# First feature and first key subtracted from a head's others, and 480 of 512 columns multiplied

## The chip, the cores and the metric

The kernel runs on one core of a Trainium2 chip. The metric is the device time of one execution in microseconds, the median of several runs. The core has TensorE (PE: matmuls, with weight loads in their own row, PEld), VectorE (DVE), ScalarE (ACT), GpSimd (POOL) and SyncE (SP, which here only issues transfers). They run side by side and wait for each other through semaphores.

## The reference

For 2048 tokens of 512 features, `x`, two branches are computed and mixed by a gate `g = sigmoid(x . gate_w)`: `g * a + (1 - g) * b`.

Branch a is a linear attention with 32 heads of 16 features, whose feature map is a pair of softmaxes:

```python
pq = jnp.einsum("bhsd,hdf->bhsf", q, w_phi)          # the same for pk
phi_q = jnp.concatenate([_softmax(pq, axis=-1), _softmax(-pq, axis=-1)], axis=-1)
kv = jnp.einsum("bhsf,bhsd->bhfd", phi_k, v)
z  = jnp.einsum("bhsf->bhf", phi_k)
o = num / den                                        # phi_q kv / (phi_q z + 1e-6), then @ wo
```

Branch b lets each of 32 heads choose one of 16 keys twice (`s1 = q1 . k1`, `s2 = q2 . k2`, the largest of each 16), which names one of 256 experts. The softmax over a single choice is 1, so the branch is `sum over heads of gelu(x . u[e]) * v[e]`.

Two facts of this arithmetic matter here. A softmax over the 16 features of a head does not change when one number is subtracted from all 16, and neither does the place of the largest of 16 scores. And q, k and the scores are linear in the weights: `x @ (w_q w_phi)`, `x @ (w_k w_phi)`, `x @ (w_q key)`.

## The kernel before

**Precision.** A matmul in the format fp32r keeps only the high part of an fp32 number, so each operand is split into a high and a low part (`h`, `l`), and one product is three matmuls: high by high, high by low, low by high (`mm3`, L52 to L57). With 512 input features in four chunks of 128, one product of a tile of 128 tokens with 512 columns is 12 matmuls that add up in one PSUM bank. `proj` (L116) makes one such product.

**Weights.** The features are folded into the weights once. `fold_k` (L225) multiplies `w_k` by `w_phi`, block by block, and `fold_turn` turns the result into `wah`, `wal`; late in the second stage `fold_q` (L207) writes the folded `w_q` over them. Both read the tile `wp`, which holds the 32 matrices `w_phi` in pairs as 32 x 32 blocks. `score_w` (L295) multiplies `w_q` of branch b by the two key tables in the tile `kp`; after a transpose by DMA the result lies in `sh`, `sl`: 1024 columns, two halves of 32 heads x 16 keys.

**Stages.** (1) Loads, folding of k, the first values. (2) k and v of the 16 tiles of tokens, and the sum `kv` over all tokens (`kvacc`). Tiles 0 to 4 and 15 are computed directly (`kproj`, `vproj`). Tiles 5 to 14 are taken in twos, with sums and differences of operands prepared on GpSimd (`Sums`), so that fewer products are needed; there the products are made by `prod` (L464), two chunks at a time, and the k of the odd tile of each two takes two calls with the folded weights (L493, L529). Between them lie the 16 calls of `score_w`, whose weights stream in from HBM. (3) Folding of q, the denominators (`z_final`). (4) One turn for each tile (`turned`, from tile 2 on): two products for the scores of the next tile (`front_s`), one for q (`front_q`), one of 258 columns for the experts and the gate (`front_p`), the masks of the chosen keys (`mid_mask`), the numerators (`mid_num`), and 18 matmuls of the output product (`back_mm`), dealt out in portions (`back_some`).

**What follows a product.** VectorE reads q and k from PSUM (`softmax_diffs`, L119): maximum and minimum over the 16 features of each head, then two differences, written to SBUF; ScalarE takes the exponential. For the scores, `best` (L729) finds the maximum of each 16 and writes a mask of where it is; the mask is transposed by DMA (`turn_eq`) and read by `mid_mask`. In all of these a head's 16 features, or keys, lie next to each other: column = 16 * head + feature.

**Order.** Every engine executes its instructions in the order in which the code issues them (`manual_schedule`); nothing is reordered. PSUM has four banks for products (`mm_bank`), taken in turn; a product can begin when the reader of the product four before it is done.

Of the kernel before, what the change touches and what calls it, by code (L numbers as in the profile page):

```python
# [16 lines left out]
ALU = mybir.AluOpType  # L17
AX = mybir.AxisListType
PSUM = bass.MemoryType.PSUM

P = 128
S = 2048
D = 512
NT = S // P
NK = D // P
H = 32
F = 16
# [7 lines left out]
def mix_kernel(ctx, tc, xT, wqT, wkT, wv, wphi, wo, wq, kk, ug, ev, cst, out):  # L35
    nc = tc.nc
    pe, dve, act, pool, sp = nc.tensor, nc.vector, nc.scalar, nc.gpsimd, nc.sync
# [11 lines left out]
        act.copy(hi, src)  # L49
        dve.tensor_tensor(lo, src, hi, op=ALU.subtract)  # L50

    def mm3(o, pairs, first=True, last=True):  # L52
        n = len(pairs)
        for i, (ah, al, bh, bl) in enumerate(pairs):
            pe.matmul(o, ah, bh, start=(first and i == 0), stop=False)  # L55
            pe.matmul(o, ah, bl, start=False, stop=False)  # L56
            pe.matmul(o, al, bh, start=False, stop=(last and i == n - 1))  # L57

    kvb = per.tile([P, 8, 32], F32, name="kvb")
    cs = per.tile([P, 160], F32, name="cs")  # L60
# [13 lines left out]
    def x_of(t):  # L74
        first = max(f for f in SEC if f <= t)
        return tuple(xt[i, first][:, t - first] for i in range(2))
# [6 lines left out]
    sh = per.tile([P, NK, 1024], F32R, name="sh")  # L83
    sl = per.tile([P, NK, 1024], F32R, name="sl")
    eh = per.tile([P, 2, D], F32R, name="eh")
    el = per.tile([P, 2, D], F32R, name="el")
    wah = per.tile([P, NK, D], F32R, name="wah")
    wal = per.tile([P, NK, D], F32R, name="wal")
# [18 lines left out]
    kp = per.tile([P, 2, 2, 32], F32, name="kp")  # L107
# [5 lines left out]
    def xs(t, k):  # L113
        return tuple(m[:, k, :] for m in x_of(t))

    def proj(o, t, wh, wl, c0, c1, ks=range(NK)):  # L116
        mm3(o, [(*xs(t, k), wh[:, k, c0:c1], wl[:, k, c0:c1]) for k in ks], ks[0] == 0, ks[-1] == NK - 1)

    def softmax_diffs(p, d, st, step=lambda: None):  # L119
        p3 = p.rearrange("p (h f) -> p h f", f=F)  # L120
        d4 = d.rearrange("p (h s f) -> p h s f", s=2, f=F)
        mx, mn = st[:, 0:32], st[:, 32:64]
        dve.tensor_reduce(mx, p3, axis=AX.X, op=ALU.max)
        step()
        dve.tensor_reduce(mn, p3, axis=AX.X, op=ALU.min)
        step()
        dve.tensor_tensor(d4[:, :, 0, :], p3, mx.unsqueeze(2).to_broadcast([P, H, F]), op=ALU.subtract)
        step()
        dve.tensor_tensor(d4[:, :, 1, :], mn.unsqueeze(2).to_broadcast([P, H, F]), p3, op=ALU.subtract)
        step()  # L130

    g64 = lambda a: a.rearrange("p (g f) -> p g f", f=F)
# [11 lines left out]
    wp = w1.tile([P, NK, 32], F32, bufs=1, name="wp")  # L144
# [14 lines left out]
    def x_high(t, ks=slice(0, NK)):  # L159
        (dve.tensor_copy if t < 3 else act.copy)(x_of(t)[0][:, ks], rawx[t][:, ks])  # L160
# [5 lines left out]
    def x_split(t, ks=slice(0, NK)):  # L166
        x_high(t, ks)
        x_low(t, ks)
# [7 lines left out]
    class Sums:  # L176
        h = ((gh, gl), x_of(NT - 1))
# [71 lines left out]
    phis, vs, pks, wsP, stk, joins = {}, {}, {}, {}, {}, []  # L249
# [19 lines left out]

    def kproj(t):  # L270
        pks[t] = mm_bank(f"pk{t}")
        proj(pks[t], t, wah, wal, 0, D)

    def k_exp(t):
        act.activation(phis[t], phis[t], AF.Exp)  # L275
# [56 lines left out]
    def front_s(t, half):  # L332
        e = st8[t]
        e[half] = mm_bank(f"s{half}_{t}")
        proj(e[half], t, sh, sl, 512 * half, 512 * half + 512)

    pool.memset(kvb, 0.0)
    tab = w1.tile([P, 1], F32, bufs=1, name="tab")
# [26 lines left out]
        split(wbh[:, k, :], wbl[:, k, :], rawv[:, k, :])  # L365
    act.dma_start(kp, kk)
    act.dma_start(cs, cst)
    x_split(1)
    dve.tensor_tensor(t2r, rawv[:, 2:4], rawv[:, 0:2], op=ALU.subtract)
    act.copy(t1r, rawv[:, 0:2])  # L370
# [90 lines left out]
            pool.tensor_tensor(t2l, t2r, t2h, op=ALU.subtract)  # L461
            pool.tensor_tensor(t4l, by4(t4r), t4h, op=ALU.subtract)

    def prod(o, left, right, first):  # L464
        for i, ((ah, al), (bh, bl)) in enumerate(zip(left, right)):
            for j, (x_, w_) in enumerate(((ah, bh), (ah, bl), (al, bh))):
                pe.matmul(o, x_, w_, start=(first and i + j == 0), stop=(i == 1 and j == 2),  # L467
                          skip_group_check=True)

    pair_of = lambda h, l, k: [(h[:, k], l[:, k]), (h[:, k + 1], l[:, k + 1])]  # L470
    b11, b21, b22 = pair_of(wah, wal, 0), pair_of(wah, wal, 2), pair_of(wbh, wbl, 2)
# [3 lines left out]
    tile_of = lambda t, k: [xs(t, k), xs(t, k + 1)]  # L475
    behind = None
    for t in range(5, NT - 1, 2):
        n = t + 1
        more = [u for u in (t + 4, t + 5) if u < NT]
        for u in more:  # L480
            x_load(u)
        if t == NT - 5:
            rawu = [spare(ug[:, 0:2], "rawu0", [P, 2, NU])]
        elif t == NT - 3:
            rawu.append(spare(ug[:, 2:4], "rawu1", [P, 2, NU]))
            rawe = [spare(ev[:, 0], "rawe0", [P, D])]
        if behind:
            k_diffs(behind)
        for u in (t + 2, t + 3):
            if u < NT - 1 and u not in (7, 9):  # L490
                x_low(u)
        a = pks[t] = mm_bank(f"pk{t}")
        prod(a, tile_of(t, 0), b11, True)  # L493
        b = mm_bank(f"pu{t}")
        act.copy(b, a)
        if 5 < t < NT - 3:
            Sums.add(t + 2)
        if t == 5:
            (j1, tp), = joins
            joins.clear()  # L500
            tj1 = wa_.tile([P, D], F32, tag="wtj", bufs=1, name="wtj1")
            join_tp(j1, tp, tj1)
            score_planes(2)
            load_wq()
            load_wq()
            join_end(j1, tj1)
            Sums.add(t + 2)
        elif t < NT - 3:
            join_all()
        else:  # L510
            (j6, tp), = joins
            joins.clear()
            tj6 = wa_.tile([P, D], F32, tag="wtj", bufs=1, name="wtj6")
            join_tp(j6, tp, tj6)
        e = tr_bank(f"pe{t}")
        prod(e, sums(0, 2), b1, True)
        prod(b, sums(1, 0), b2, False)
        c = mm_bank(f"pv{t}")
        act.copy(c, b)
        if t == 5:  # L520
            k_exp(4)
            k_sum(4)
            k_mult(4)
            x_high(9)
            (j2, tp), = joins
            joins.clear()
            tj2 = wa_.tile([P, D], F32, tag="wtj", bufs=1, name="wtj2")
            join_tp(j2, tp, tj2)
        prod(a, tile_of(t, 2), b21, False)  # L529
        k_diffs(t)  # L530
        if behind:
            k_exp(behind)
            k_sum(behind)
            k_mult(behind)
        score(2, 5 < t < NT - 3)
        if t == NT - 3:
            rawq = stage(wqT, "rawq")
            score_planes(7)
        elif t > 5:
            load_wq()  # L540
            load_wq()
        for u in (t - 3, t - 2):
            kvacc(u)
        vn, vt = v_tile(n), v_tile(t)
        if t > 5:
            act.copy(vn, by16(e))
            k_exp(t)
            k_sum(t)
        prod(b, sums(0, 0), b3, False)
        d = pks[n] = mm_bank(f"pk{n}")  # L550
        act.copy(d, b)
        if t == 5:
            join_high(j2, tj2)
            score_planes(3)
            act.copy(vn, by16(e))
            Sums.high(7, (0,))
            k_exp(t)
            x_low(9)
        prod(c, sums(1, 2), b22, False)
        if t == 5:  # L560
            Sums.high(7, (1,))
        if t == NT - 3:
            x_split(NT - 1)
        dve.tensor_tensor(vt, by16(c), vn, op=ALU.add)
        dve.tensor_tensor(vn, by16(b), vn, op=ALU.add)
        if t == 5:
            k_sum(t)
        o2 = d.rearrange("p (c n) -> p c n", c=2)
        prod(o2, tile_of(n, 2), b4, False)
        if t + 3 < NT:  # L570
            if t > 5:
                Sums.high(t + 2)
            Sums.low(t + 2)
            if t == 5:
                join_low(j2, tj2)
        if t == 7:
            for i in range(2):
                x_parts(i, 11)
        for u in more if n < NT - 4 else ():
            if u != 9:  # L580
                x_high(u)
        k_mult(t)
        behind = n
    t = NT - 1
# [36 lines left out]
    def step(t, n=1):  # L621
        for _ in range(n):
            if t in chains and next(chains[t], None) is None:
                del chains[t]
# [47 lines left out]

    def front_q(t):
        pq = mm_bank(f"pq{t}")
        proj(pq, t, wah, wal, 0, D)
        st8[t]["pq"] = pq

    def soft_in(t, step=lambda: None):
# [51 lines left out]
    def best(t, half):  # L730
        e = st8[t]
        if half == 0:
            e["eq"] = w2.tile([P, 1024], BF16, tag="eq", name=f"eq{t}")
        p3 = e[half].rearrange("p (h f) -> p h f", f=F)
        mx = w2.tile([P, 32], F32, tag="mx", name=f"mx{half}_{t}")
        dve.tensor_reduce(mx, p3, axis=AX.X, op=ALU.max)  # L736
        dve.tensor_tensor(e["eq"][:, 512 * half:512 * half + 512].rearrange("p (h f) -> p h f", f=F), p3,  # L737
                          mx.unsqueeze(2).to_broadcast([P, H, F]), op=ALU.is_equal)

    def turn_eq(t):  # L740
        e = st8[t]
# [332 lines left out]
    for a in range(NT - 1):  # L1074
        n, b, z = a + 1, a - 1, a - 2
# [61 lines left out]
    a, b, z = NT - 1, NT - 2, NT - 3  # L1137
# [140 lines left out]
```

## Time and profile before

| | |
|---|---|
| median of 3 runs | 366.96 us (366.78 to 367.57) |
| profiled execution | 367.09 us |
| its span, first to last instruction | 365.3 us |
| TensorE, matmuls | 358.8 us busy, 98% of the span |
| VectorE | 318.5 us, 87% |
| ScalarE | 256.7 us, 70% |
| GpSimd | 206.6 us, 57% |
| granted TensorE clock | 0.999 |

Matmuls are pipelined: a listed matmul of 512 columns lasts about 0.39 us, but the next one starts about 0.23 us after it, so the start-to-start distance is what a matmul costs. A row of a timeline reads: start, duration, engine, line, operation, output<-inputs, shape; in brackets the idle time before it and what ended that. A row of waits reads: engine, its tile and line, what it waited for, then microseconds in total, number of times, the longest. In a group of instructions, "x128 | 50.4, 394 | 0.0" is count, total busy us, mean ns of one, idle us before them.

### The profile page before, as it was taken

What the parts mean: (1) busy time and instruction counts of PE and PEld (TensorE: products, weight loads), DVE (VectorE), ACT (ScalarE), POOL (GpSimd) and SP (SyncE); (2) the same over time, 40 slices, a digit from 0 to 9 for tenths busy, and PEclk for the clock granted to TensorE, in tenths of its full rate; (3) what the DMA queues carried; (4) which work ended last, traced back from release to release, by engine and by line L of the source; (5) the groups of instructions that cost most, each with busy time, mean ns of one, the idle gap of its engine ahead of it and who ended that gap; (6) DMA issues with size and microseconds to landing.
All of it is one profiled execution on the core that took longest, in us unless ns stands there. A gap on an engine that the chain in (4) does not pass through costs nothing.

```text
span 365.3 us, 8628 instructions
## 1 busy us (share of the span) xinstructions
PE 358.8 (98%) x3404; PEld 282.2 (77%) x3404; DVE 318.5 (87%) x639; ACT 256.7 (70%) x455; POOL 206.6 (57%) x205
## 2 busy tenths in 40 slices
PE   7999999999999999999999999999999999999996
PEld 3766667777778878887888888888888888888764
DVE  3679999999968889999999799699899899699791
ACT  4586577977566666695786876866769787667882
POOL 1079989988938947446337355634734635636130
PEclk9999999999999999999999999999999999999999
DMA  7868787459693112243471344263344245145233
GB/s 254 321 237 304 241 274 248 137 210 309 206 247 99 57 38 51 39 100 45 101 117 43 88 86 90 57 104 65 80 86 102 50 111 101 46 88 129 31 100 117
DMA packets 75752, 47.57 MB, mean 130 GB/s; under 512 B 67264, under 2 KB 68160, under 8 KB 73408
## 3 DMA queue, kind: packets, MB, share of 16 engines
q1 hardware_dynamic: 74848, 46.15, 46.8%
q10 hardware_dynamic: 864, 0.87, 0.9%
q8 instruction: 27, 0.44, 0.5%
q14 instruction: 13, 0.11, 0.1%
HBM read 26.43 MB, written 4.19 MB: 84 GB/s over the span
## 4 chain that ended last, share of the span: by engine, by line
PE 86%; ACT 5%; POOL 3%; DMA 2%; DVE 2%; issue 1%; SPq 0%; POOLq 0%; ACTq 0%; DVEq 0%
PE po L889 9%; PE s L55 7%; PE s L56 7%; PE s L57 7%; PE pk L467 5%; PE po L896 5%; PE pu L467 4%; PE ws L300 4%; PE pq L55 4%; PE pq L56 4%; PE pq L57 4%; PE oT L776 2%; PE kvacc L291 2%; PE pp L55 2%; PE pp L56 2%; PE pp L57 2%
## 5 line engine op out<-in xcount | busy, mean ns | idle before, releaser
L728 POOL TENSOR_TENSOR d<-d,st 128x512 f32<-128x512 f32 x30 | 32.6, 1106 | 49.3 <-DVE st L721 48.1
L699 POOL TENSOR_TENSOR w<-d,zb 128x512 f32<-128x512 f32 x32 | 41.2, 1310 | 18.7 <-ACT d L693 18.7
L55 PE MATMUL s<-sh,xh 128*128 128x512 f32 x128 | 50.4, 394 | 0.0
L56 PE MATMUL s<-sl,xh 128*128 128x512 f32 x128 | 49.9, 389 | 0.0
L57 PE MATMUL s<-sh,xl 128*128 128x512 f32 x128 | 49.8, 389 | 0.0
L757 ACT COPY pl<-d 128x1024 uint16<-128x1024 uint16 x32 | 33.3, 1046 | 18.7 <-POOL d L728 18.7
L768 ACT COPY ptb<-tp 128x1024 uint16<-128x1024 uint16 x32 | 41.7, 1370 | 0.4 <-DMA tp<-pl 0.4
L284 POOL TENSOR_TENSOR d<-d,st 128x1024 f32<-128x1024 f32 x16 | 32.6, 2036 | 8.5 <-ACT d L275 6.5
L844 POOL TENSOR_TENSOR cf<-cf,px 128x256 f32<-128x256 f32 x15 | 11.1, 741 | 33.6 <-DVE cf L840 31.8
L55 PEld LDWEIGHTS s<-sh,xh 128*128 128x128 f32 x128 | 24.0, 188 | 5.3 <-issue 0.4
L57 PEld LDWEIGHTS s<-sh,xl 128*128 128x128 f32 x128 | 24.0, 188 | 5.1
L56 PEld LDWEIGHTS s<-sl,xh 128*128 128x128 f32 x128 | 24.0, 188 | 4.8
L55 PE MATMUL pq<-wah,xh 128*128 128x512 f32 x64 | 25.2, 393 | 0.0
L57 PE MATMUL pq<-wah,xl 128*128 128x512 f32 x64 | 24.9, 390 | 0.0
L56 PE MATMUL pq<-wal,xh 128*128 128x512 f32 x64 | 24.9, 389 | 0.0
L703 DVE TENSOR_REDUCE st<-d 128x32 f32<-128x512 f32 x32 | 20.5, 678 | 3.6 <-ACT d L693 3.5
L164 DVE TENSOR_TENSOR xl<-xr,xh 128x512 fp32r<-128x512 f32 (+2 forms) x17 | 21.7, 1292 | 1.7 <-ACT xh L160 1.6
L737 DVE TENSOR_TENSOR eq<-s,mx 128x512 bf16<-128x512 f32 x32 | 22.1, 692 | 1.1
L736 DVE TENSOR_REDUCE mx<-s 128x32 f32<-128x512 f32 x32 | 21.8, 680 | 0.2 <-PE s L57 0.2
L707 DVE TENSOR_REDUCE st<-w 128x32 f32<-128x512 f32 x32 | 20.5, 676 | 0.9 <-POOL w L699 0.9
L279 DVE TENSOR_REDUCE st<-d 128x64 f32<-128x1024 f32 x16 | 19.4, 1210 | 1.8 <-ACT d L275 1.6
L927 ACT COPY ot<-po 128x512 f32<-128x512 f32 x15 | 8.7, 589 | 16.3 <-PE po L896 14.8
(271 smaller groups left out, 1097.1 us busy)
## 6 DMA issues: line engine op xcount, KB each, us to landing
wq<-wq SPq DMA_DIRECT2D x16, 1024.0 KB, 5.2
xr<-xT SPq DMA_DIRECT2D x15, 256.0 KB, 5.1
y<-ot SPq DMA_DIRECT2D x15, 256.0 KB, 2.0
rawk<-wkT SPq DMA_DIRECT2D x1, 1024.0 KB, 6.8
rawq<-wqT SPq DMA_DIRECT2D x1, 1024.0 KB, 6.8
rawu<-ug SPq DMA_DIRECT2D x2, 258.0 KB, 5.5
rawv<-wv ACTq DMA_DIRECT2D x2, 256.0 KB, 4.7
rawv<-wv SPq DMA_DIRECT2D x2, 256.0 KB, 6.0
```

The lines of the kernel that those rows point to most:

```text
L55: pe.matmul(o, ah, bh, start=(first and i == 0), stop=False)
L56: pe.matmul(o, ah, bl, start=False, stop=False)
L57: pe.matmul(o, al, bh, start=False, stop=(last and i == n - 1))
L284: pool.tensor_tensor(g64(d), g64(d), b64(st[:, 128:192]), op=ALU.mult)
L467: pe.matmul(o, x_, w_, start=(first and i + j == 0), stop=(i == 1 and j == 2), skip_group_check=True)
L699: pool.tensor_tensor(hs(e["w"], i), hs(e["ph"], i), hs(zb, i), op=ALU.mult)
L728: eng.tensor_tensor(g64(d)[:, gs_], g64(d)[:, gs_], r[:, gs_].unsqueeze(2).to_broadcast([P, 32, F]), op=ALU.mult)
L736: dve.tensor_reduce(mx, p3, axis=AX.X, op=ALU.max)
L737: dve.tensor_tensor(e["eq"][:, 512 * half:512 * half + 512].rearrange("p (h f) -> p h f", f=F), p3, mx.unsqueeze(2).to_broadcast([P, H, F] ...
L757: act.copy(pl, e["ph"][:, halves[i]].bitcast(U16).rearrange("p (c j) -> p j c", j=2))
L768: act.copy(p16[:, t % 2, :, 4 * i:4 * i + 4, :], st8[t]["tp"][i].rearrange("p (j g) n -> p j g n", j=2))
L889: pe.matmul(po, a, b, start=(i == 0), stop=False)
```

## The change

The tile `wp` and the key table `kp` are altered on GpSimd right after they are loaded, ahead of the folds: the first feature (key) of each head is subtracted from the head's other 15 and is itself set to zero (`from_first`). The folded weights of q, k and the scores then have a column of zeros for each head, and every other column is the difference to it.

The heads are interleaved in twos, so that the two zero columns of two heads lie side by side: column = 32 * pair + 2 * feature + head in the pair. The host writes `w_phi` and the keys in that order, and VectorE reads PSUM through a rearranged view with a step of two (`heads`); what it writes to SBUF keeps the old order, and so does everything behind it.

`live` selects the 480 columns that are not zero: 16 runs of 30, with two columns left out between them. In each accumulation the first matmul still takes all 512, which writes the zeros; the others take 480, in the moving operand and in the output. This holds for `front_s`, `front_q`, `kproj`, and the two `prod` calls with the folded weights of an odd tile.

```diff
-    def mm3(o, pairs, first=True, last=True):
+    def mm3(o, pairs, first=True, last=True, live=lambda a: a):
         n = len(pairs)
         for i, (ah, al, bh, bl) in enumerate(pairs):
-            pe.matmul(o, ah, bh, start=(first and i == 0), stop=False)
-            pe.matmul(o, ah, bl, start=False, stop=False)
-            pe.matmul(o, al, bh, start=False, stop=(last and i == n - 1))
+            whole = first and i == 0
+            f = (lambda a: a) if whole else live
+            pe.matmul(f(o), ah, f(bh), start=whole, stop=False, skip_group_check=True)
+            pe.matmul(live(o), ah, live(bl), start=False, stop=False, skip_group_check=True)
+            pe.matmul(live(o), al, live(bh), start=False, stop=(last and i == n - 1), skip_group_check=True)
+
+    def from_first(w):
+        g = w.rearrange("p a (f i) -> p a f i", i=2)
+        pool.tensor_tensor(g[:, :, 1:], g[:, :, 1:], g[:, :, 0:1].to_broadcast([P, 4, F - 1, 2]), op=ALU.subtract)
+        pool.memset(g[:, :, 0:1], 0.0)
+
+    def live(a):
+        return a.rearrange("p (g f) -> p g f", f=2 * F)[:, :, 2:]
+
+    def heads(a):
+        return a.rearrange("p (g f i) -> p g i f", f=F, i=2)
+
+    twice = lambda a: a.rearrange("p (g i) -> p g i", i=2)
+    spread = lambda a: twice(a).unsqueeze(3).to_broadcast([P, F, 2, F])
...
     def softmax_diffs(p, d, st, step=lambda: None):
-        p3 = p.rearrange("p (h f) -> p h f", f=F)
-        d4 = d.rearrange("p (h s f) -> p h s f", s=2, f=F)
+        p4 = heads(p)
+        d5 = d.rearrange("p (g i s f) -> p g i s f", i=2, s=2, f=F)
...
-        dve.tensor_reduce(mx, p3, axis=AX.X, op=ALU.max)
+        dve.tensor_reduce(twice(mx), p4, axis=AX.X, op=ALU.max)
...
-        dve.tensor_tensor(d4[:, :, 0, :], p3, mx.unsqueeze(2).to_broadcast([P, H, F]), op=ALU.subtract)
+        dve.tensor_tensor(d5[:, :, :, 0, :], p4, spread(mx), op=ALU.subtract)
...
-        proj(pks[t], t, wah, wal, 0, D)
+        proj(pks[t], t, wah, wal, 0, D, live=live)
...
-        proj(e[half], t, sh, sl, 512 * half, 512 * half + 512)
+        proj(e[half], t, sh, sl, 512 * half, 512 * half + 512, live=live)
...
     act.dma_start(kp, kk)
     act.dma_start(cs, cst)
+    from_first(wp)
+    from_first(kp.rearrange("p a b c -> p (a b) c"))
     x_split(1)
...
-    def prod(o, left, right, first):
+    def prod(o, left, right, first, live=lambda a: a):
         for i, ((ah, al), (bh, bl)) in enumerate(zip(left, right)):
             for j, (x_, w_) in enumerate(((ah, bh), (ah, bl), (al, bh))):
-                pe.matmul(o, x_, w_, start=(first and i + j == 0), stop=(i == 1 and j == 2),
+                whole = first and i + j == 0
+                f = (lambda a: a) if whole else live
+                pe.matmul(f(o), x_, f(w_), start=whole, stop=(i == 1 and j == 2),
                           skip_group_check=True)
...
-        prod(a, tile_of(t, 0), b11, True)
+        prod(a, tile_of(t, 0), b11, True, live)
...
-        prod(a, tile_of(t, 2), b21, False)
+        prod(a, tile_of(t, 2), b21, False, live)
...
-        proj(pq, t, wah, wal, 0, D)
+        proj(pq, t, wah, wal, 0, D, live=live)
...
-        p3 = e[half].rearrange("p (h f) -> p h f", f=F)
+        p4 = heads(e[half])
...
-        dve.tensor_reduce(mx, p3, axis=AX.X, op=ALU.max)
-        dve.tensor_tensor(e["eq"][:, 512 * half:512 * half + 512].rearrange("p (h f) -> p h f", f=F), p3,
-                          mx.unsqueeze(2).to_broadcast([P, H, F]), op=ALU.is_equal)
+        dve.tensor_reduce(twice(mx), p4, axis=AX.X, op=ALU.max)
+        dve.tensor_tensor(e["eq"][:, 512 * half:512 * half + 512].rearrange("p (g i f) -> p g i f", i=2, f=F), p4,
+                          spread(mx), op=ALU.is_equal)
...
-        wphi[j:j + F, h // 8, j % 32:j % 32 + F] = ph[h]
+        wphi[j:j + F, h // 8, h % 2::2] = ph[h]
...
-        kk[:, h, 0, :F], kk[:, h, 1, F:] = k_, k_
+        kk[:, h, 0, 0::2], kk[:, h, 1, 1::2] = k_, k_
```

More of the change, by code (lines that the diff above doesn't have):

```diff
@@ L114, in xs, with proj @@
         return tuple(m[:, k, :] for m in x_of(t))
-    def proj(o, t, wh, wl, c0, c1, ks=range(NK)):
-        mm3(o, [(*xs(t, k), wh[:, k, c0:c1], wl[:, k, c0:c1]) for k in ks], ks[0] == 0, ks[-1] == NK - 1)
+    def proj(o, t, wh, wl, c0, c1, ks=range(NK), live=lambda a: a):
+        mm3(o, [(*xs(t, k), wh[:, k, c0:c1], wl[:, k, c0:c1]) for k in ks], ks[0] == 0, ks[-1] == NK - 1, live)
     def softmax_diffs(p, d, st, step=lambda: None):
-        p3 = p.rearrange("p (h f) -> p h f", f=F)
-        d4 = d.rearrange("p (h s f) -> p h s f", s=2, f=F)
+        p4 = heads(p)
+        d5 = d.rearrange("p (g i s f) -> p g i s f", i=2, s=2, f=F)
         mx, mn = st[:, 0:32], st[:, 32:64]
-        dve.tensor_reduce(mx, p3, axis=AX.X, op=ALU.max)
+        dve.tensor_reduce(twice(mx), p4, axis=AX.X, op=ALU.max)
         step()
-        dve.tensor_reduce(mn, p3, axis=AX.X, op=ALU.min)
+        dve.tensor_reduce(twice(mn), p4, axis=AX.X, op=ALU.min)
         step()
-        dve.tensor_tensor(d4[:, :, 0, :], p3, mx.unsqueeze(2).to_broadcast([P, H, F]), op=ALU.subtract)
+        dve.tensor_tensor(d5[:, :, :, 0, :], p4, spread(mx), op=ALU.subtract)
         step()
-        dve.tensor_tensor(d4[:, :, 1, :], mn.unsqueeze(2).to_broadcast([P, H, F]), p3, op=ALU.subtract)
+        dve.tensor_tensor(d5[:, :, :, 1, :], spread(mn), p4, op=ALU.subtract)
         step()
```

## The prediction

> **What bounds the kernel now.** I read the page first: its span, its first table and the chain of work that ended last.
>
> ```profile
> span 365.3 us, 8628 instructions
> PE 358.8 (98%) x3404; PEld 282.2 (77%) x3404; DVE 318.5 (87%) x639; ACT 256.7 (70%) x455; POOL 206.6 (57%) x205
> PE 86%; ACT 5%; POOL 3%; DMA 2%; DVE 2%; issue 1%; SPq 0%; POOLq 0%; ACTq 0%; DVEq 0%
> ```
>
> TensorE sets the time, but 14% of the chain runs over other engines, and VectorE has little room. So I looked at what a matmul costs by its start-to-start distance (the timeline of TensorE; first and last of 24 score matmuls, then of 12 gate matmuls of 258 columns), because the listed durations overlap.
>
> ```profile
> 264.40 0.39 PE L55 MATMUL s<-sh,xh 128*128 128x512 f32 x1
> 269.62 0.39 PE L57 MATMUL s<-sh,xl 128*128 128x512 f32 x1
> ...
> 259.31 0.28 PE L55 MATMUL pp<-uh,xh 128*128 128x258 f32 x1
> 260.64 0.29 PE L57 MATMUL pp<-uh,xl 128*128 128x258 f32 x1
> ```
>
> 512 columns: (269.62-264.40)/23 = 0.2270 us. 258 columns: (260.64-259.31)/11 = 0.1209 us. A column is worth (0.2270-0.1209)/254 = 0.418 ns, and 32 columns less are worth 13.4 ns of matmul.
>
> Next, the stages: busy time of each engine in four stretches (stretch, its length, then PE, PEld, DVE, ACT, POOL).
>
> ```profile
> 21.00:49.00 28.00, 28.00 (x267) 19.03 (x265) 25.03 (x29) 18.93 (x26) 27.76 (x16) 1.00 0.77 265
> 139.30:201.30 62.00, 62.00 (x468) 50.70 (x468) 59.57 (x152) 44.49 (x85) 31.71 (x34) 1.00 0.39 73
> ...
> 243.00:338.00 95.00, 95.00 (x676) 79.47 (x674) 87.63 (x200) 70.60 (x131) 47.68 (x48) 1.00 0.38 85
> ```
>
> TensorE is full in all three, but in the first GpSimd is as full (27.76 of 28.00), and in the second VectorE has 2.43 us of 62 left. There a faster TensorE only waits, once its margin is used up. In the third VectorE has 7.37 of 95 left.
>
> **The change, part by part.**
>
> *Matmuls that get shorter.* From the groups by shape, one row for each kind:
>
> ```profile
> L55 PE MATMUL s<-sh,xh 128*128 128x512 f32 x128 | 50.4, 394 | 0.0
> L55 PE MATMUL pq<-wah,xh 128*128 128x512 f32 x64 | 25.2, 393 | 0.0
> L55 PE MATMUL pk<-wah,xh 128*128 128x512 f32 x24 | 9.6, 398 | 0.0
> L467 PE MATMUL pk<-wah,xh 128*128 128x512 f32 x20 | 7.9, 395 | 0.0
> L467 PE MATMUL pk<-sh,xh 128*128 128x512 f32 x10 | 3.9, 389 | 0.0
> ```
>
> Each stands for three rows of equal count (high by high, high by low, low by high). Of every 12 in a call of `proj` one keeps 512 columns, and so does the first of the 12 in the two `prod` calls of an odd tile: scores 384-32 = 352, q 192-16 = 176, k direct 72-6 = 66, k of odd tiles 60-5 = 55. That is 649 matmuls, 649 x 13.4 ns = 8.7 us if all arrive. The last row (even tiles) stays at 512.
>
> *What a broken pattern costs.* The 480 columns are 16 runs of 30 with two left out between them, in the moving operand and in the output. The trace has only a pattern of two runs of 256 (the last row above): 6 of them, then 6 unbroken ones.
>
> ```profile
> 57.58 0.39 PE L467 MATMUL pk<-sh,xh 128*128 128x512 f32 x1
> ...
> 58.94 0.39 PE L467 MATMUL pk<-wah,xh 128*128 128x512 f32 x1
> ...
> 60.30 0.39 PE L467 MATMUL pe<-t1h,gh 128*128 128x512 f32 x1
> ```
>
> Both sixes took 1.36 us, so one break costs less than 0.01/6 us = 1.7 ns. For 15 breaks that leaves 0 to 25 ns against the 13.4 saved. A gain from a break is excluded: nothing is computed less. I take 0, since the nearest row shows no difference at all, and keep both ends for the range. [...]
>
> *VectorE reads PSUM at a step of two.* The maxima, minima, differences and equalities (L123 to L129, L736, L737) keep their element counts but read every second fp32. The nearest rows: a cast that hops 64 bytes from element to element (L808), and reads that don't hop.
>
> ```profile
> L808 DVE CAST sa<-mk 128x128 uint16<-128x128 f32 x6 | 1.7, 280 | 0.0
> L808 DVE CAST sa<-mk 128x64 uint16<-128x64 f32 x4 | 0.9, 214 | 0.0
> ...
> L789 DVE TENSOR_TENSOR xl<-oT,xh 128x256 fp32r<-128x256 f32 x32 | 11.9, 415 | 4.6 <-ACT xh L783 4.6
> L736 DVE TENSOR_REDUCE mx<-s 128x32 f32<-128x512 f32 x32 | 21.8, 680 | 0.2 <-PE s L57 0.2
> ```
>
> With hops (280-214)/64 = 1.03 ns an element, without (680-415)/256 = 1.04 ns. I take 0; the other end, half speed, would add 512 x 1.04 = 0.53 us to each of 192 instructions (8 in a tile of the last stage, 4 in a tile of k).
>
> *GpSimd's four new instructions.* Each `from_first` is a subtraction of 120 elements and a small memset, on GpSimd, waiting for a load.
>
> ```profile
> 13.19 0.21 POOL L392 CAST wm<-cs 128x32 bf16<-128x32 f32 x1 [11.52 <-DMA cs<-cst]
> 20.94 2.38 POOL L394 TENSOR_TENSOR xraw<-xraw,xraw 128x1024 f32<-128x1024 f32 x1 [7.54 <-ACT xraw L246]
> ...
> 8.31 0.33 ACTq L366 DMA_DIRECT2D kp<-kk  x1
> ...
> kp<-kk ACTq DMA_DIRECT2D x1, 64.0 KB, 4.6
> ```
>
> A subtraction lies between the 0.21 us of 32 elements (first row) and the 2.38 us of 1024; near the first end, some 0.4 us. The second waits for the keys until 8.31+4.6 = 12.9 us, and queued behind it are the ones of `v` for three tiles and L392; all are done by about 14.5. GpSimd then idles until 20.94, so it costs nothing; without that cover about 1.3 us. The copy into `v` writes other columns and waits for TensorE alone. No DMA is added or moved.
>
> **Where the gain is lost.** *(a) Until 61 us:* 71 of the short matmuls (0.95 us) lie there. GpSimd is dense from 20.94 on, and TensorE already waits for it, at 49 and at 61 us:
>
> ```profile
> PEld pu L467 <- POOL xl L197: 0.4, 1, 0.4
> PEld pe L467 <- POOL gl L197: 0.4, 1, 0.4
> ```
>
> I keep 0. *(b) 61 to 109 us:* 39 of them, 0.52 us, kept (0.5). *(c) 109 to 133.5 us:* the chain in order of time leaves TensorE and comes back to it through the denominators:
>
> ```profile
> 107.85 1.17 PE pv L467 x5
> 109.09 0.63 ACT xh L160
> ...
> 128.87 2.41 POOL zsum L955
> 131.31 0.63 ACT zh L967
> 131.96 0.70 DVE zl L968
> 132.71 0.50 PE z L939
> ```
>
> 55 short matmuls (0.73 us) lie beside it: keep 0. *(d) 133.5 to 202 us:* 176 of them, 2.35 us, but VectorE is dense. TensorE may run ahead only until it meets what VectorE frees. The tightest place is the masks of tile 5, behind a transpose of the equality tile:
>
> ```profile
> 197.85 0.69 DVE L737 TENSOR_TENSOR eq<-s,mx 128x512 bf16<-128x512 f32 x1
> 198.62 1.23 SPq L743 DMA_TRANSPOSE et<-eq  x1
> ...
> 201.86 0.48 PE L798 MATMUL mk<-wm,et 128*128 128x16 bf16 x13
> ...
> et<-eq SPq DMA_TRANSPOSE x16, 2.7
> ```
>
> The transpose lands at 198.62+2.7 = 201.3, 0.6 us ahead of its reader: keep 0.6. *(e) 202 to 243 us:* 99 of them, 1.32 us; at 243.32 TensorE already waits for VectorE's `cl`, whose work began with the q of that tile; the two score calls between (22 matmuls, 0.29 us) are lost:
>
> ```profile
> 243.32 0.30 PEld L896 LDWEIGHTS po<-eh,cl 128*128 128x128 f32 x2 [0.42 <-DVE cl L877]
> ```
>
> Keep 1.0. *(f) 243 to 338 us:* 209 of them, 2.79 us. VectorE itself waits for TensorE's q in this part (its waits from 201 us on, 5.2 us in 5 times), so it follows:
>
> ```profile
> DVE st L123 <- PE pq L57: 5.2, 5, 1.5
> ```
>
> Keep 2.8. After 338 there are none, and that tail moves as a whole. Sum: 0.5+0.6+1.0+2.8 = 4.9 us of 8.7. The profiled execution took 367.09 us (365.3 of span and 1.8 around it), 0.13 over the median of 366.96: 367.09-4.9 = 362.2, and about **362.1** against the median.
>
> **The rivals.** *All of it arrives:* the waits have more room than their margins show; 367.0-8.7 = 358.3. Against it are the waits that already exist at 49, 133 and 243 us. *Half:* a break costs about one column, 0.42 x 15 = 6 ns; half the sum of (b), (e), (f) and the 0.6 of (d), 2.8 us, so 364.2. *No shorter:* a matmul of 480 takes what one of 512 takes, because a break costs two columns or the operand is fetched in whole pieces of 16 bytes, of which a run that begins two columns late still touches as many. The change would then not do what it says: 367.0. *Slower, by the breaks:* place, the same 649 matmuls; the point from which it decides is 13.4/15 = 0.9 ns a break, and four columns a break (1.7 ns, the most that the two-run rows allow) cost 25-13.4 = 11.7 ns each, +7.6 us, 374.6. Nothing hides it where TensorE is full. [...] *Slower, by VectorE:* in 139 to 201 us it has 2.43 us left over some four and a half tiles of 8 such reads, 36, so 0.07 us a read is enough to make it the bound; at half speed 318.5+192 x 0.53 = 420 us of VectorE, some 425 in all. [...]
>
> **How the numbers follow.** The forecast with 4.9 us of gain has 0.58, and its own range of 360.0 to 364.0 (waits in (a) to (e) kept or lost). All 0.04, half 0.12, no shorter 0.10, slower by breaks 0.09, slower by VectorE 0.07. A measurement of this kernel tells about 0.2% (0.73 us) from no change. Faster: 0.58+0.04+0.12 = 0.74; same 0.10; slower 0.16. The range 359.4 to 367.6 leaves out the two slower cases (0.16) and the whole gain (0.04).
>
> **What would show it.** Right: scores, q and k 480 wide start 0.2136 us after each other; L736, L737 and L123 stay at about 680 ns; the stretch from 21 to 49 us keeps its length and the wait of L467 for L197 grows from 0.4 to over 1 us; TensorE gets waits for masks or banks before 202 us; two tiles of the last stage take 66 x 13.4 ns = 0.9 us less. Wrong: a distance over 0.227 us (breaks), L736 well over 680 ns (steps), GpSimd late at 20.94.

## The result

The changed kernel takes **368.94 us** (median of 10 runs, 368.37 to 369.97), the kernel before took 367.01 us beside it (10 runs, 366.52 to 368.16). The ratio is 1.0052, 95% interval 1.0039 to 1.0064: 1.9 us slower, where 4.9 us less was forecast, and outside the range of 359.4 to 367.6.

The page of the changed kernel, the lines that answer to those of before (span, busy times, shares of the chain that ended last):

```profile
span 367.4 us, 8632 instructions
...
PE 360.7 (98%) x3404; PEld 282.3 (77%) x3404; DVE 319.0 (87%) x639; ACT 256.4 (70%) x455; POOL 208.8 (57%) x209
...
PE 81%; DVE 6%; ACT 6%; POOL 3%; DMA 2%; issue 2%; ACTq 0%; POOLq 0%; DVEq 0%
```

TensorE is as dense as before and 1.9 us longer busy, though 649 of its matmuls multiply 480 columns and not 512. The groups by shape (count, busy us, mean ns of one, idle us before) show them no shorter: 394 ns, where the same row of 512 columns had 389. The first pair is that row before and after the change, the second pair VectorE's equality before and after, then its maximum after; after the change VectorE reads with a step of two:

```profile
L56 PE MATMUL s<-sl,xh 128*128 128x512 f32 x128 | 49.9, 389 | 0.0
L58 PE MATMUL s<-sl,xh 128*128 128x480 f32 x128 | 50.4, 394 | 0.0
...
L737 DVE TENSOR_TENSOR eq<-s,mx 128x512 bf16<-128x512 f32 x32 | 22.1, 692 | 1.1
L757 DVE TENSOR_TENSOR eq<-s,mx 128x512 bf16<-128x512 f32 x32 | 22.1, 691 | 1.1
L756 DVE TENSOR_REDUCE mx<-s 128x32 f32<-128x512 f32 x32 | 21.7, 680 | 0.2 <-PE s L59 0.2
```

What counts is the distance from start to start. These are the 24 score matmuls of one tile, the same as those taken before (timeline of TensorE, first of the first call, its second and last, and last of the second call):

```profile
265.81 0.39 PE L57 MATMUL s<-sh,xh 128*128 128x512 f32 x1
266.04 0.39 PE L58 MATMUL s<-sl,xh 128*128 128x480 f32 x1
...
268.37 0.40 PE L59 MATMUL s<-sh,xl 128*128 128x480 f32 x1
...
271.13 0.39 PE L59 MATMUL s<-sh,xl 128*128 128x480 f32 x1
```

Over the 24 it is (271.13-265.81)/23 = 231.3 ns, and between the 480s of the first call (268.37-266.04)/10 = 233 ns; before it was 227.0. Over the whole kernel the mean distance behind the row L58, all 128 of it, is 230.5 ns: 3.5 ns too much, times 649 is 2.3 us, against 1.9 to 2.1 us lost (medians, spans). So the loss has about the size of the longer matmuls, and nothing else needs to have got slower. What made them longer is the question of the runs.

### The profile page after: what moved, and what is told of

Its sections match the earlier page's. It is cut to its first block, busy times and chain, and to the rows that moved or that the text cites. A ratio compares the mean times of both kernels' runs of the same rounds, so it can differ in the third digit from the quotient of the medians.

```text
span 367.4 us, 8632 instructions
## 1 busy us (share of the span) xinstructions
PE 360.7 (98%) x3404; PEld 282.3 (77%) x3404; DVE 319.0 (87%) x639; ACT 256.4 (70%) x455; POOL 208.8 (57%) x209
## 4 chain that ended last, share of the span: by engine, by line
PE 81%; DVE 6%; ACT 6%; POOL 3%; DMA 2%; issue 2%; ACTq 0%; POOLq 0%; DVEq 0%
PE po L909 9%; PE s L57 8%; PE s L58 8%; PE s L59 8%; PE po L916 5%; PE pk L487 4%; PE pq L57 4%; PE pq L58 4%; PE pq L59 4%; PE pu L487 3%; PE oT L796 2%; DVE xl L180 2%; PE pp L57 2%; PE pp L58 2%; PE pp L59 2%; PE ws L316 2%
## 5 line engine op out<-in xcount | busy, mean ns | idle before, releaser
L57 PE MATMUL s<-sh,xh 128*128 128x480 f32 (+1 forms) x128 | 50.9, 398 | 0.0
L58 PE MATMUL s<-sl,xh 128*128 128x480 f32 x128 | 50.4, 394 | 0.0
L59 PE MATMUL s<-sh,xl 128*128 128x480 f32 x128 | 50.4, 394 | 0.0
L777 ACT COPY pl<-d 128x1024 uint16<-128x1024 uint16 x32 | 33.2, 1043 | 17.5 <-POOL d L748 17.5
L57 PEld LDWEIGHTS s<-sh,xh 128*128 128x128 f32 x128 | 24.1, 188 | 5.6 <-DVE d L143 0.2
L58 PEld LDWEIGHTS s<-sl,xh 128*128 128x128 f32 x128 | 24.1, 189 | 5.1
L57 PE MATMUL pq<-wah,xh 128*128 128x512 f32 (+1 forms) x64 | 25.4, 397 | 0.0
L58 PE MATMUL pq<-wal,xh 128*128 128x480 f32 x64 | 25.2, 394 | 0.0
L59 PE MATMUL pq<-wah,xl 128*128 128x480 f32 x64 | 25.1, 393 | 0.0
```

The lines of the kernel that those rows point to most:

```text
L57: pe.matmul(f(o), ah, f(bh), start=whole, stop=False, skip_group_check=True)
L58: pe.matmul(live(o), ah, live(bl), start=False, stop=False, skip_group_check=True)
L59: pe.matmul(live(o), al, live(bh), start=False, stop=(last and i == n - 1), skip_group_check=True)
L777: act.copy(pl, e["ph"][:, halves[i]].bitcast(U16).rearrange("p (c j) -> p j c", j=2))
```

## The experiments

**Theories**, none of them shown by a row so far. A: each break of a pattern costs a fixed time, about 1 ns (an estimate: 230.5 ns, less the 213.6 forecast, over 15 breaks). B: the moving operand (here the weights, whose columns are those of the output) costs time as if it were fetched in whole pieces of 16 bytes, that is aligned groups of four columns; a run of columns costs every piece that it touches, and a run of 30 that begins two columns late touches eight, as many as 32 columns do. C: the breaks of the output in PSUM cost it. D: not the matmuls, but VectorE's stepped reads or GpSimd's subtractions.

**1. Matmuls alone, one pattern after another.** A kernel of its own, with groups of 24 matmuls back to back into one bank, of which each group has its own pattern:

```diff
+    def go(name, mov, dst=None):
+        o = bank(name)
+        o_ = (dst or mov)(o)
+        for i in range(N):
+            pe.matmul(o_, x[:, i % 4, :], mov(w[:, (i // 2) % 4, :]), start=(i == 0), stop=(i == N - 1), skip_group_check=True)
```

> Groups of 24 fp32r matmuls alone on TensorE, one group for each pattern; the rest of the computation is left out and the output holds other numbers. Theory A (a break costs time by itself, about 2.3 columns = 0.95 ns): unbroken 480 at 0.213 us, 16 runs of 30 at 0.227 to 0.230, 8 of 60 at 0.220, 4 of 120 at 0.217, 2 of 240 at 0.215, 16 of 28 at about 0.214, 16 of 24 at 0.188. Theory B (the moving operand is fetched in pieces of 16 bytes, so a run that begins 8 bytes into a piece costs as if it were whole): 16 of 30 at 0.227, but 8 of 60, 4 of 120, 2 of 240 and 16 of 28, all of which begin on a piece, cost only their columns (0.213 for 480, 0.200 for 448). Theory C (the write to PSUM is what breaks): the pattern in the output alone costs like both, the pattern in the moving operand alone costs like unbroken 480; by B it is the other way round.

The timeline of TensorE, one execution at a granted clock of 1.00, shows each group as one row (start, length of the whole row of 24; the last digits of a group's name are left out, and the shape tells 16 runs of 28, 448 columns, from 16 runs of 30):

```profile
25.86 5.34 PE L49 MATMUL c480off<-w,x 128*128 128x480 f32 x24
31.03 5.75 PE L49 MATMUL both16x<-w,x 128*128 128x480 f32 x24
36.62 5.76 PE L49 MATMUL mov16x<-w,x 128*128 128x480 f32 x24
42.22 5.36 PE L49 MATMUL out16x<-w,x 128*128 128x480 f32 x24
47.42 5.61 PE L49 MATMUL tail16x<-w,x 128*128 128x480 f32 x24
52.86 5.34 PE L49 MATMUL both8x<-w,x 128*128 128x480 f32 x24
58.04 5.44 PE L49 MATMUL both4x<-w,x 128*128 128x480 f32 x24
...
68.52 5.12 PE L49 MATMUL both16x<-w,x 128*128 128x448 f32 x24
73.48 5.03 PE L49 MATMUL c<-w,x 128*128 128x448 f32 x24
...
89.59 5.64 PE L49 MATMUL last<-w,x 128*128 128x512 f32 x24
```

The length less the last matmul's own duration (0.34 to 0.40 us, from the groups), over 23, is the distance:

| pattern of 480 columns | ns |
|---|---|
| unbroken from column 2 (c480off) | 215.7 |
| 16 runs of 30, two left out ahead of each, in both operands (both16x): the change | 232.8 |
| the same in the moving operand alone (mov16x) | 233.2 |
| the same in the output alone (out16x) | 216.6 |
| 16 runs of 30, two left out behind each (tail16x) | 227.0 |
| 8 runs of 60, four left out ahead of each (both8x) | 215.7 |
| 4 runs of 120, eight left out ahead of each (both4x) | 219.9 |
| 2 runs of 240, sixteen left out ahead of each (both2x) | 216.6 |

and 448 columns are 206.6 ns as 16 runs of 28 that begin on a piece, 202.8 unbroken; 512 unbroken are 226.7 in the first group (start to start in the trace) and 228.2 in the last. C falls: 15 breaks of the output cost 0.9 ns together (216.6 against 215.7). The whole cost is in the moving operand: 233.2 ns with the pattern there alone, 232.8 with it in both. A (a fixed cost per break) falls as the cause: 7 breaks at multiples of four columns cost nothing (215.7 and 215.7), 15 of them 3.8 ns (206.6 against 202.8), and 15 others 11 ns or 17 ns by where the runs begin (227.0 and 232.8 against 215.7). The 3 breaks of the runs of 120 cost 4.2 ns, more than the 7 of the runs of 60, although those runs begin and end on a piece too; neither A nor B has a reason for that, and it stays open.

**2. Where the runs begin, and how long they are.** The same kernel with other patterns, each of them in the moving operand and in the output alike:

```diff
+    go("at0len28", lambda a: cut(a, 28, 4, False))
+    go("at2len28", lambda a: a.rearrange("p (g f) -> p g f", f=32)[:, :, 2:30])
+    go("at4len28", lambda a: cut(a, 28, 4, True))
...
+    go("at0len30", lambda a: cut(a, 30, 2, False))
+    go("at2len30", lambda a: cut(a, 30, 2, True))
```

> Groups of 24 matmuls as before, patterns of 16 (or 8) runs in the moving operand and output; the rest is left out. Theory B (16-byte pieces of 4 columns): a run costs four columns for each piece it touches. Runs of 28 from column 0 or 4 touch 7 pieces, 0.207 us as measured; runs of 28 from column 2 touch 8, so 0.227 or more; runs of 26 from column 0 or 6 touch 7, so 0.207 and not the 0.187 of plain 416; 8 runs of 62 touch 16, so 0.227 from column 0, over 0.227 from column 2; 8 of 60 0.216. Theory A (a fixed cost for a break, whatever its place): runs of 28 the same from 0, 2 and 4; runs of 26 about 0.20; 8 of 62 about 0.228 less 2 columns, both ways.

The timeline again; the name says at which column of its 32 (or 64) a run begins, and the shape how long the 16 (or 8) runs are, 448 being runs of 28:

```profile
15.61 5.60 PE L49 MATMUL whole<-w,x 128*128 128x512 f32 x24
21.05 5.13 PE L49 MATMUL at0len<-w,x 128*128 128x448 f32 x24
26.02 5.61 PE L49 MATMUL at2len<-w,x 128*128 128x448 f32 x24
31.47 5.12 PE L49 MATMUL at4len<-w,x 128*128 128x448 f32 x24
36.43 5.12 PE L49 MATMUL at0len<-w,x 128*128 128x416 f32 x24
41.39 5.16 PE L49 MATMUL at6len<-w,x 128*128 128x416 f32 x24
46.39 5.62 PE L49 MATMUL at0len<-w,x 128*128 128x480 f32 x24
51.84 5.76 PE L49 MATMUL at2len<-w,x 128*128 128x480 f32 x24
57.43 5.61 PE L49 MATMUL at0len62x<-w,x 128*128 128x496 f32 x24
62.88 5.79 PE L49 MATMUL at2len62x<-w,x 128*128 128x496 f32 x24
```

Runs of 28 have as many columns and breaks in all three rows. Begun at column 0 or 4 they touch seven pieces and take 207.0 and 206.5 ns; begun at column 2 they touch eight and take 227.0, what 512 columns take (226.6). Runs of 26 touch seven pieces from column 0 and from column 6, and take 206.4 and 208.1, no less than runs of 28, where 416 unbroken columns take 188.4 (start to start in the trace). Runs of 30 touch eight either way: 227.4 and 233.2. So B holds in the main: **the time goes by the pieces touched, not by the columns used**, but for up to 4 ns (207.0 against 202.8 for 448 unbroken) and the part below. Only fp32r was tried, so whether a piece is 16 bytes or four elements isn't told apart; nor do these rows show how the operand is fetched, only how long a matmul takes.

One part is not explained, and the loss itself lies in it, since by the pieces alone the change would have cost nothing: runs of 30 or 62 from column 2, which begin in mid-piece and end on a piece's end, take 6 to 8 ns more than the same runs from column 0, with as many pieces. Runs of 28 from column 2, which begin and end in mid-piece, don't, and runs of 26 from column 6, which end on a piece's end, take only 1.7 ns more.

**3. The change with all 512 columns.** Zero columns, interleaving, subtractions and stepped reads stay; only the patterns are whole again:

```diff
     def live(a):
-        return a.rearrange("p (g f) -> p g f", f=2 * F)[:, :, 2:]
+        return a
```

> The changed kernel with all matmuls at 512 columns again (subtraction, zero columns, interleaving and the stepped reads of VectorE stay). If the whole loss is in the broken matmuls: 367.0, the time of before, within 0.7. If the stepped reads or GpSimd's new instructions cost the 1.9 us: 368.9.

367.00 us (10 runs, 366.55 to 367.23), ratio to the kernel before 0.9999 (0.9989 to 1.0008). D falls: all that the change does beside the patterns is free, within 0.1%, and the whole loss is in the broken patterns of the matmuls.

**4. 480 columns unbroken.** The last 32 columns are left out of all but the first matmul of a call, in place of the zero columns, so that sums of two heads in 32 are incomplete:

```diff
     def live(a):
-        return a.rearrange("p (g f) -> p g f", f=2 * F)[:, :, 2:]
+        return a[:, :D - 32]
```

> The changed kernel with 480 unbroken columns in place of the 16 runs: the last 32 columns are left out of the sums, so q, k and scores of the last two heads are wrong. It has the forecast's shorter matmuls without breaks. By the prediction's account of the waits: 4.9 us less than before, 362.1. If all of the 8.7 us arrives: 358.3. If VectorE and GpSimd hold more of it back than the margins say: 364 to 366.

362.45 us (4 runs, 362.07 to 363.60), ratio 0.9881 (0.9864 to 0.9899). With the columns side by side the matmuls do get shorter (378 or 379 ns in the rows of 394), and the kernel gains 4.5 us. In the list of TensorE's waits (us in all, times, longest) three that the prediction named now open or grow (`xl` of GpSimd at 48.7 us, `et`, `zl`), and the longest is one that it didn't name, 1.2 us for VectorE's `xl` at 111.5 us:

```profile
PE pk L59 <- DVE xl L180: 1.2, 1, 1.2
...
PE pu L487 <- POOL xl L213: 0.7, 1, 0.7
PE mk L818 <- DMA et<-eq: 0.5, 1, 0.5
...
PE z L959 <- DVE zl L988: 0.2, 1, 0.2
```

**5. Zero columns at the end of a run.** Feature and key 15 are subtracted in place of feature and key 0, so the runs of 30 begin on a piece; the 480 columns and the 15 breaks stay:

```diff
-        pool.tensor_tensor(g[:, :, 1:], g[:, :, 1:], g[:, :, 0:1].to_broadcast([P, 4, F - 1, 2]), op=ALU.subtract)
-        pool.memset(g[:, :, 0:1], 0.0)
+        pool.tensor_tensor(g[:, :, :F - 1], g[:, :, :F - 1], g[:, :, F - 1:].to_broadcast([P, 4, F - 1, 2]), op=ALU.subtract)
+        pool.memset(g[:, :, F - 1:], 0.0)
...
-        return a.rearrange("p (g f) -> p g f", f=2 * F)[:, :, 2:]
+        return a.rearrange("p (g f) -> p g f", f=2 * F)[:, :, :30]
```

> The changed kernel with the last feature and key subtracted in place of the first, so that the runs of 30 begin on a 16-byte piece and end 8 bytes short of one; same counts otherwise. Theory B: such a matmul takes what 512 columns take, 0.2268 us, so the time of before, 367.0 within 0.6. Theory A (cost of a break, wherever it lies): as the changed kernel, 368.9.

367.95 us (10 runs, 367.38 to 368.06), ratio 1.0015 (1.0004 to 1.0025): the time of before but for 0.15%, as B has it, and 1 us less than the change, with which it shares the number of breaks. The mean distance behind L58 is 227.7 ns, where it was 227.0 before, and 0.7 ns times 649 is 0.5 us, about what is left (0.6 us by the ratio, 0.8 by the medians).

**6. The live columns packed.** B says what a version needs that gains: the 480 columns side by side in SBUF, while the output, whose 15 breaks cost 0.9 ns, keeps its 16 runs of 30. The casts that make the high parts and the subtractions that make the low ones write packed; the first chunk's high part keeps 512 columns, for the matmul that writes the zeros:

```diff
-            pe.matmul(live(o), ah, live(bl), start=False, stop=False, skip_group_check=True)
+            pe.matmul(fit(o, bl), ah, bl, start=False, stop=False, skip_group_check=True)
...
+    def fit(o, b):
+        return live(o) if len(b.shape) == 3 and b.shape[2] == R else o
...
     def join_high(j, tj):
-        act.copy(sh[:, :, P * j:P * j + P], tj.rearrange("p (k e) -> p k e", k=NK))
+        act.copy(sh[:, 0, P * j:P * j + P], tj[:, :P])
+        act.copy(at_pack(sh, j)[:, 1:], tj.rearrange("p (k c i) -> p k c i", k=NK, c=4)[:, 1:, :, 2:])
...
+    def at_pack(w, j):
+        c0 = 512 * (j // 4) + 4 * R * (j % 4)
+        return w[:, :, c0:c0 + 4 * R].rearrange("p k (c i) -> p k c i", c=4)
```

> The changed kernel with the 480 live columns of the weights stored side by side (only the high part of the first chunk keeps 512, for the two matmuls that read it): no breaks in the moving operand, the output keeps its 16 runs of 30 in PSUM, VectorE reads as in the changed kernel. Theory B: the output's breaks cost nothing, so 10 of 12 matmuls take 0.2165 us, 59 calls x 10 x 10.2 ns = 6.0 us less, of which e_contig's share (4.5 of 6.6) arrives, 4.1 us: 362.9, within 1. If the output's breaks cost something in the kernel after all: 366 to 369. The four added instructions for each packing are worth under 0.5 us in all.

370.51 us (6 runs, 369.26 to 373.59), ratio 1.0111 (1.0075 to 1.0147): the slowest of all, although its 480s are nearly as short as those of experiment 4 (row L57 below, 381 ns with a stall ahead of it and the slow stretch behind it). The groups, then TensorE's timeline at the first score call:

```profile
L57 PE MATMUL s<-sl,xh 128*128 128x480 f32 x128 | 48.8, 381 | 2.7 <-POOL sl L364 2.7
L56 PE MATMUL s<-sh,xh 128*128 128x480 f32 (+1 forms) x128 | 50.0, 390 | 0.6 <-ACT sh L358 0.6
```

```profile
116.36 0.37 PE L58 MATMUL s<-sh,xl 128*128 128x480 f32 x1
117.36 0.48 PE L56 MATMUL s<-sh,xh 128*128 128x480 f32 x1 [0.62 <-ACT sh L358]
120.56 0.49 PE L57 MATMUL s<-sl,xh 128*128 128x480 f32 x1 [2.72 <-POOL sl L364]
```

This call reads the groups 0 to 3; the split it waits for is that of group 7, on GpSimd from 119.22 to 120.50. The first two chunks pass and the third waits. The stretches from the stall on (length, then PE, PEld, DVE, ACT, POOL, and the granted clock):

```profile
118.00:120.00 2.00, 0.00 (x0) 0.00 (x0) 1.49 (x3) 0.35 (x1) 2.00 (x3) 1.00 0.21 66
120.00:122.00 2.00, 1.44 (x9) 1.02 (x9) 0.00 (x0) 0.00 (x0) 2.00 (x3) 0.97 0.00 0
122.00:124.00 2.00, 2.00 (x41) 2.00 (x44) 0.00 (x0) 0.00 (x0) 0.98 (x1) 0.50 0.00 0
124.00:126.00 2.00, 2.00 (x72) 1.94 (x76) 0.00 (x0) 0.50 (x2) 0.00 (x0) 0.50 0.00 0
126.00:128.00 2.00, 2.00 (x102) 1.86 (x95) 1.84 (x6) 2.00 (x8) 0.00 (x0) 0.50 0.03 8
```

After idle times of 0.62 and 2.72 us, with one matmul of 0.48 us between them, the granted clock was 0.50 for 6 us, in which TensorE lost about 3 more (an estimate: half of the 6): the stall was paid about twice. Experiment 7, which has no such stall, shows a granted clock of 1.00 in every stretch from 109 to 130 us. What it takes to lower the clock this one stall does not show.

**7. Packed, with a tile for each half of the heads.** If group 7 was waited for only because it lies in the same tile, two tiles take the wait away:

```diff
-    sh = per.tile([P, NK, 1024], F32R, name="sh")
-    sl = per.tile([P, NK, 1024], F32R, name="sl")
+    sh = [per.tile([P, NK, 512], F32R, name=f"sh{i}") for i in range(2)]
+    sl = [per.tile([P, NK, 512], F32R, name=f"sl{i}") for i in range(2)]
...
-        proj_packed(e[half], t, sh, sl, 512 * half)
+        proj_packed(e[half], t, sh[half], sl[half])
```

> The packed kernel again, with the score weights of the two halves of the heads in two tiles each (sh0, sh1, sl0, sl1) in place of one; nothing else differs. In the packed kernel the first score matmuls of tile 0 (the half that reads groups 0 to 3) waited from 116.5 to 120.5 us for the split of group 7, whose columns they do not read; the wait began at the third chunk, where the stretch of memory from the first to the last element that the split writes first covers the columns read. TensorE then stood idle and its granted clock was 0.50 from 122 to 128 us. If that wait is between neighbours in one tile (theory): it goes with the two tiles, the clock stays at 1.00, and ten of twelve matmuls a call are 10.2 ns shorter: 59 calls x 10 x 10.2 ns = 6.0 us, of which the unbroken kernel kept 4.55 of 6.6, so some 4.1 of them: 362.9 us (362.0 to 364.5). If the stall comes from the added packing work on ScalarE and GpSimd being late (rival): the wait at 116.5 stays and the time stays near 370.5. If a packed weight makes the matmuls with 16 runs of 30 in their output slower over a whole kernel than alone (a second rival, which the group alone at 216.5 ns speaks against): between 365 and 367.

**363.49 us** (6 runs, 362.68 to 363.82), ratio to the kernel before 0.9895 (0.9865 to 0.9924). It computes all that the reference does and beats both kernels: 3.4 us under the one before (366.92 beside it). The same place of the timeline (the third chunk), and the group:

```profile
116.43 0.38 PE L56 MATMUL s<-sh,xh 128*128 128x480 f32 x1
116.66 0.37 PE L57 MATMUL s<-sl,xh 128*128 128x480 f32 x1
```

```profile
L57 PE MATMUL s<-sl,xh 128*128 128x480 f32 x128 | 48.5, 379 | 0.0
```

The added casts and subtractions of the packing hold TensorE up nowhere by 0.2 us or more: the list of its waits, which goes down to that, names neither `sh` nor `sl`. The wait was one between neighbours in a tile. Why the order kept between writes and reads took them for the same columns is not shown. The stretch from a write's first to its last element would fit experiment 6 (the split of group 7 writes chunks 1 to 3 in one instruction, and that stretch covers chunks 2 and 3 of group 0). But in the kernel before, the same split wrote all four chunks in one instruction,

```profile
119.15 1.27 POOL L324 TENSOR_TENSOR sl<-wtj,sh 128x512 fp32r<-128x512 f32 x1
```

a stretch that covers chunks 1 to 3 of group 0, and the score call read those of `sl` from 116.19 us on, ahead of the split and without a wait. So the stretch alone is not the rule. The packed write also has a pattern of three steps (chunk, pair of heads, column) where that one has two; this was not tried by itself.

## Why the prediction was wrong

**The step that failed** is the price of a broken pattern: "For 15 breaks that leaves 0 to 25 ns against the 13.4 saved. [...] I take 0, since the nearest row shows no difference at all". The bounds held: 15 breaks cost 233.2-215.7 = 17.5 ns alone, and 230.5-217.9 = 12.6 ns in the kernel (the row L58 against the same row of experiment 4), where 32 columns less save 227.0-217.9 = 9.1. The choice between the bounds did not hold. The nearest row, two runs of 256, is near in form but not in what matters: its runs begin and end on pieces of 16 bytes, so it could only show that such a break is nearly free (under 1.7 ns), as those of 8 runs of 60 are too (215.7 ns, and 215.7 unbroken). The row speaks of breaks; the cost is in the main one of alignment, 16 half-used pieces, and for the rest (227.4 to 233.2 ns) one of a beginning in mid-piece that is not explained.

**The right account stood among the rivals.** "No shorter" named the operand "fetched in whole pieces of 16 bytes, of which a run that begins two columns late still touches as many" and gave it 0.10 and 367.0 us. The times of experiments 2 and 5 go by such pieces in the main (207.0, 227.0 and 206.5 ns for runs of 28 from columns 0, 2 and 4; how the operand is fetched, no run shows), and experiment 5 is that rival nearly to its time. The change itself came out 1.9 us above it, by what its runs of 30 from column 2 cost beyond their pieces: 3.5 ns a matmul in the kernel, 6 alone. The rival "slower, by the breaks" had the right side, and the wrong law: it would have made experiment 5 as slow as the change and left 8 runs of 60 slower than 480 in one.

**The saving of a matmul was too large.** A slope from 258 to 512 columns gave 0.418 ns a column, 13.4 for 32. Unbroken 480 took 216.5 ns against 226.7 (start to start in the trace of experiment 1, from column 0): 10.2 ns, a quarter less. Distances are not a straight line in the columns here (448: 202.8, so another 13.7 for the next 32).

**The account of waits held in the main.** It could be tested only once the matmuls did get shorter. 649 x 10.2 ns = 6.6 us, of which experiment 4 kept 4.5 us; the prediction kept 4.9 of 8.7 and ended at 362.1, experiment 4 at 362.45: two misses that nearly cancel, a smaller saving and a larger share of it kept, so that the nearness of the two times is luck. Place by place, in experiment 7 (starts, against 132.71, 201.86, 243.32 and 329.70 of before; the first two rows are of before, then four of experiment 7):

```profile
201.86 0.56 PE L798 MATMUL mk<-wm,et 128*128 128x16 bf16 x16
329.70 0.39 PE L57 MATMUL pq<-wah,xl 128*128 128x512 f32 x1
...
132.58 0.50 PE L989 MATMUL z<-zl,neg 128*128 128x512 f32 x1 [0.22 <-DVE zl L1018]
...
201.08 0.36 PE L848 MATMUL mk<-wm,et 128*128 128x16 bf16 x8 [0.42 <-DMA et<-eq]
...
241.49 0.61 PE L946 MATMUL po<-eh,cl 128*128 128x512 f32 x2
...
326.25 0.38 PE L58 MATMUL pq<-wah,xl 128*128 128x480 f32 x1
```

- (a) to (c): at the denominators the gain is 0.1 us. TensorE waits for VectorE's `zl`, as forecast; but the 0.5 us kept from (b) did not outlast that wait.
- (d): the masks of tile 5 wait for the equality tile's transpose, the place named. The wait comes at the ninth of 16 matmuls, which starts at 201.08; before, the 16 began at 201.86 and took 0.56 us, the ninth at some 202.1, an estimate from these two numbers. That is 1.0 us earlier, and 0.5+0.6 were forecast.
- (e): 1.8 us ahead at `cl`, forecast 2.1. The wait of 0.42 us there is gone, so the two calls counted as lost weren't.
- (f): another 1.6 us by the last q, forecast 2.8; 209 matmuls at 10.2 ns, of which experiment 7 shortens 10 in 11, are 1.9.

**VectorE's step of two** was taken as 0: 680 and 691 ns after, 680 and 692 before. These rows show no cost for fp32 read from PSUM at a step of 8 bytes, and so, with experiment 3, the rival of 425 us falls; the half speed that it is added up from is in no run.

**GpSimd's new instructions** were put at 0.4 us each and done by 14.5 us. In GpSimd's timeline of the changed kernel:

```profile
7.77 0.60 POOL L63 TENSOR_TENSOR wp<-wp 128x120 f32<-128x120 f32 x1 [6.30 <-DMA wp<-wphi]
...
13.03 0.49 POOL L63 TENSOR_TENSOR kp<-kp 128x120 f32<-128x120 f32 x1 [4.50 <-DMA kp<-kk]
...
13.80 0.88 POOL L410 CAST wm<-cs 128x32 bf16<-128x32 f32 x1
20.98 2.39 POOL L412 TENSOR_TENSOR xraw<-xraw,xraw 128x1024 f32<-128x1024 f32 x1 [6.31 <-ACT xraw L262]
```

0.5 to 0.6 us each, done at 14.68, and the next instruction waits for ScalarE until 20.98, as before (20.94).

## What to carry to other kernels

Count the aligned groups of four columns that an fp32r moving operand touches, not the columns that are multiplied: here 28 columns of every 32 took 207.0 ns from column 0 and 227.0 from column 2, where all 512 took 226.6. So pack the live columns side by side where the weights are written (216.5 ns for 480), and let the gaps stand in the output (0.9 ns for 15). When a price is taken from the nearest row, ask what that row would look like under each rival; here one that begins and ends on 16 bytes could not tell a cost of alignment from none. And when a tile is written by more, smaller or stepped pieces, look for new waits between its halves: here one cost 7 us (370.51 against 363.49) and a second tile took it away.

## What was not expected of the hardware

- 15 breaks in the PSUM output of a matmul cost at most 0.9 ns together (216.6 against 215.7 ns).
- An fp32r moving operand costs the aligned groups of four columns that it touches: 16 runs of 28 columns of 32 take 207.0, 206.5 or 227.0 ns, begun at column 0, 4 or 2.
- Runs of 30 or 62 columns from column 2 take 6 to 8 ns more than the same runs from column 0 (233.2 to 227.4); why stays open.
- 4 runs of 120 columns take 4.2 ns more than 8 runs of 60 (219.9 to 215.7); why stays open.
- Idle times of 0.62 and 2.72 us close together in a dense kernel were followed by a granted clock of 0.50 for 6 us.
